# Softmax-normalisation hooks moved one or two steps later, and the second layer norm's pass on GpSimd in two of four blocks

## Chip, cores and metric

The kernel runs on one core of a Trainium2 chip. The metric is device time in microseconds (us), the median of several executions. A separate execution was recorded by the hardware profiler; durations below come from that one.

## What is computed

A transformer block whose two layer norms are modulated by a condition vector `c`, with attention of 32 query heads that share one key and one value head, and a bilinear feed-forward network:

```python
mod = silu(c) @ w_mod                       # six rows: sa, ca, ga, sb, cb, gb
h = layernorm(x) * (1 + ca) + sa
q = h @ wq (32 heads of 16);  k = h @ wk;  v = h @ wv
p = softmax(q k^T / 4);  o = p v
x = x + ga * (o @ wo)
h = layernorm(x) * (1 + cb) + sb
x = x + gb * (((h @ w_gate) * (h @ w_up)) @ w_down)
```

There are 2048 tokens, 512 model columns and 1792 feed-forward columns, all float32.

## The kernel before, in words

**Blocks and units.** The tokens are cut into four blocks of 512 queries (b = 0 to 3). In a block the 32 heads are done four at a time, so a block has 8 units and the program 32 (u = 0 to 31, g = u mod 8). A unit goes over 16 key tiles of 128 keys. One key tile is a *turn*, and a turn has two half-turns; the hooks that are called in them have the index i, 0 to 31 in a unit.

**What a turn does.** Four score products (`sc`, L631) whose exponentials ScalarE writes (`P`, L633); four score products of a later unit for the row maximum (`mx`, L581) that VectorE reduces (`mpart`, L584); and, one turn late, eight accumulating products of P with the values (`pv`, L642; the four heads of a pair of key tiles share the array by column groups). Eight PSUM banks are handed round among all of these.

**Side work.** In what is left of TensorE's time, half-height products are put between the others, in one row group of the array while `sc` or `mx` uses the other (`side`, L499): first the query projections of the later blocks (four slots in a turn, called FEW), then, from unit 8 on, the output projection (`wo`) and the feed-forward products of the block before (eight slots in a turn, called MANY). Where a `side` group changes its row group, its product waits, by a dependency written by hand, for an exponential of the turn before.

**Softmax normalisation.** When two units (8 heads) are done, their sums of exponentials lie in DRAM (`rs`). `normalise` then has three steps: `load` (SP reads the sums as a 128x32 tile `rc`, L664), `recip` (VectorE takes reciprocals, L667; SP writes them to DRAM as `ri`, L669, and reads them back, spread over the partitions, as `rr`, L671), and `mult` (GpSimd multiplies the head outputs `oc` by `rr`, L676, and splits the product into two float16 halves `och`, L678 and L679). `hooks` calls these in units with g in (0, 3, 4, 6), at i = 4, 8 and 14. The last group of the last block is normalised after the attention.

**Second layer norm.** Early in the next block (units 8 and 9, 16 and 17, 25 and 26) four `wo` groups, one for each token tile t of 128 tokens, end one after the other. At each end VectorE adds the residual (`x`, L724), takes statistics (`bs`, L732) and combines them (`st`, L735); GpSimd makes the reciprocal deviation in six tiny operations (`ry`, L190 to L195) and in two more the bias `nb` (L737, L738). After the fourth tile, the pass that writes the normalised tile (`n2`, here shown as `n`, L742) is called for t = 0 to 3 after 2, 4, 6 and 9 ticks in the later blocks, and the transposes (`mx`, L771), whose evictions are `hf` (L778), from tick 11 on. Two ticks make a turn. The pass is a ScalarE activation, n2 = y*x + nb.

**Order.** The program is written out in one order for all engines; each engine takes its own instructions in that order, and waits at one whose input or buffer isn't ready while everything behind it on that engine waits too. GpSimd also prepares the feed-forward weights (`wsl`, `kwb`, `wg`, `wu`, `wd`; L903 to L1010) until unit 11 or so, and splits the feed-forward products (`glu`, L824 and L825).

Of the kernel before, what the change touches and what calls it, by code (L numbers as in the profile page):

```python
# [15 lines left out]
AF = mybir.ActivationFunctionType  # L16
OP = mybir.AluOpType
# [22 lines left out]
CHANNEL = {0: KC - 1, 3: 0, 4: 1, 6: 2}  # L40
# [13 lines left out]
def adaln_mqa_glu_kernel(ctx: ExitStack, tc: tile.TileContext, x_in, wq_in, wk_in, wv_in, wo_in,  # L54
                         wg_in, wu_in, wd_in, c_in, wm_in, out):
    nc = tc.nc
# [140 lines left out]
    def rstd_of(st, n):  # L197
        y = work.tile([128, 4], F32, name="ry", bufs=6)[:, :n]
        rstd_into(y, st[:, :, 1], n)
        return y  # L200
# [487 lines left out]
    def after(delay, f):  # L688
        if tick[0] is None:
            f()  # L690
        else:
            timers.setdefault(tick[0] + delay, []).append(f)
# [6 lines left out]
    def load_x(b, t):  # L699
        xl = work.tile([128, D], F32, name="xl", tag="xl", bufs=3)  # L700
        r0 = b * BT + t * 128
        nc.sync.dma_start(xl, x_rows[r0:r0 + 128, :])
        xls[b, t] = xl

    def wo_work(b):
        def op(t):
            def f(i):
                ch, term = divmod(i, 3)
                ol, wl = TERMS[term]
                return och[b, ch][:, ol, t * 128:(t + 1) * 128], wo[:, wl, ch, :]  # L710
            return f

        def pre(t):
            def f():
                load_x(b, t)
            return f

        def fin(t):
            def f(p):
                if b < NB - 1:  # L720
                    x1 = work.tile([128, D], F32, name="x1", tag="x1", bufs=6)
                else:
                    x1 = work.tile([128, D], F32, name="x1p", tag="P", bufs=8)
                nc.vector.scalar_tensor_tensor(x1, p, sca[:, 7:8], xls[b, t], op0=OP.mult, op1=OP.add)  # L724
                x1s[b, t] = x1
                s2 = work.tile([128, 1, 2], F32, name="st2", bufs=5)
                bs = work.tile([128, 6], F32, name="bs", bufs=4)
                nb = work.tile([128, 2], F32, name="nb", bufs=4)
                yt = {}

                def spread():
                    nc.vector.bn_stats(bs, x1)  # L732

                def aggr():
                    nc.vector.bn_aggr(s2[:, 0, :], bs)  # L735
                    yt["y"] = rstd_of(s2, 1)
                    nc.gpsimd.tensor_tensor(nb[:, 0:1], s2[:, 0, 0:1], yt["y"], op=OP.mult)  # L737
                    nc.gpsimd.tensor_scalar(nb[:, 1:2], nb[:, 0:1], -1.0, 0.0, op0=OP.mult, op1=OP.add)  # L738

                def nrm():  # L740
                    n2 = work.tile([128, D], F32, name="n2", tag="och", bufs=4)
                    nc.scalar.activation(n2, x1, AF.Identity, bias=nb[:, 1:2], scale=yt["y"])  # L742
                    n2s[b, t] = n2

                after(3, spread)
                after(4, aggr)
                n2f[b, t] = nrm
                if t == 3:
                    for j, d in enumerate((2, 4, 6, 9) if b else (2, 4, 7, 12)):
                        after(d, n2f[b, j])  # L750
                    if b < NB - 1:
                        after(TR_WAIT if b else TR_WAIT + 3, lambda: turns.extend(ln2_work(b)))
            return f

        return [Group(3 * KC, op(t), fin(t), pre(t)) for t in range(4)]
# [5 lines left out]
    def ln2_work(b):  # L761
        items = []
        st = {}

        def tr(k):
            def f():
                if k == 0:
                    h2s[b] = big.tile([128, 2, KC, BT], F16, name="h2T", tag="wq")
                st["p"] = ps_hold("mx")
                for t in range(4):  # L770
                    nc.tensor.transpose(st["p"][:, t * 128:(t + 1) * 128], n2s[b, t][:, k * 128:(k + 1) * 128],  # L771
                                        ident)
            return f

        def ev(k):
            def f():
                hf = work.tile([128, BT], F32, name="hf", tag="g", bufs=2)
                nc.scalar.activation(hf, st["p"], AF.Identity, bias=hsc[:, k, 0:1], scale=hsc[:, k, 1:2])  # L778
                ps_give(st["p"])
                eng = nc.vector if b == NB - 1 else nc.gpsimd  # L780
                eng.tensor_scalar(h2s[b][:, 0, k, :], hf, 1.0, 0.0, op0=OP.mult, op1=OP.add)
                eng.tensor_tensor(h2s[b][:, 1, k, :], hf, h2s[b][:, 0, k, :], op=OP.subtract)
                if k == KC - 1:
                    h2done.add(b)
            return f

        for k in range(KC):
            items.append((900, tr(k), ev(k)))
        return items
# [310 lines left out]
    def side_step(step):  # L1100
        if side and step >= side_next[0] and (step % 2 or side[0][1] is nothing):
            gap, f, post = side.popleft()
            side_next[0] = max(side_next[0], step) + gap
            f()
            if post:
                posts.append(post)
# [26 lines left out]
    nrm = []  # L1133
# [16 lines left out]
    def attend(u, kt):  # L1150
# [9 lines left out]
        for turn in range(2):  # L1160
# [31 lines left out]
            if not late_max() and turns:  # L1192
                _, f, post = turns.popleft()
                f()
                posts.append(post)
            hooks(u, 2 * (kt + turn) + 1)

    def hooks(u, i):
        b, g = divmod(u, UB)
        step = u * NSTEP + i  # L1200
        side_step(step)
        if u > 0 and g in CHANNEL and i in (4, 8, 14):
            if i == 4:
                nrm[:] = normalise(b - (g == 0), CHANNEL[g])
            nrm[(4, 8, 14).index(i)]()
        if i == 16 and u > 0 and g == 0:
            left = list(fill)
            fill.clear()
            gu, down = ffn_work(b - 1)
            early = max(len(left) - 2, 0)  # L1210
            fill.extend(left[:early])
            fill.extend(([step + 4], w) for w in wo_work(b - 1))
            fill.extend(left[early:])
            fill.extend((["h2", b - 1], w) for w in gu + down)
# [14 lines left out]
    u = NU - 1  # L1229
# [28 lines left out]
    nrm = normalise(NB - 1, KC - 1)  # L1258
# [33 lines left out]
```

## Time and profile before

| What | us |
|---|---|
| Time, median of 3 runs (1699.13 to 1699.99) | 1699.75 |
| The profiled execution's own time | 1698.53 |
| Its span, first to last instruction | 1696.5 |
| TensorE matmul busy | 1653.9 |
| VectorE busy | 1392.2 |
| ScalarE busy | 1220.1 |
| GpSimd busy | 506.3 |

Rows of the profile give an engine's instructions in order of time: start, duration, engine, line, operation, output<-input, shapes and count, and in brackets how long the engine was idle just before and what released it. Grouped rows give busy time and the mean in ns of one instruction, then idle time. A wait row gives total us, number of times and the longest. Runs of equal instructions are merged in a timeline into one row, which starts with the first of them.

### The profile page before, as it was taken

What the parts mean: (1) busy time and instruction counts of PE and PEld (TensorE: products, weight loads), DVE (VectorE), ACT (ScalarE), POOL (GpSimd) and SP (SyncE); (2) the same over time, 40 slices, a digit from 0 to 9 for tenths busy, and PEclk for the clock granted to TensorE, in tenths of its full rate; (3) what the DMA queues carried; (4) which work ended last, traced back from release to release, by engine and by line L of the source; (5) the groups of instructions that cost most, each with busy time, mean ns of one, the idle gap of its engine ahead of it and who ended that gap; (6) DMA issues with size and microseconds to landing.
All of it is one profiled execution on the core that took longest, in us unless ns stands there. A gap on an engine that the chain in (4) does not pass through costs nothing.

```text
span 1696.5 us, 33291 instructions
## 1 busy us (share of the span) xinstructions
PE 1653.9 (97%) x12709; PEld 535.1 (32%) x12709; DVE 1392.2 (82%) x2364; ACT 1220.1 (72%) x2295; POOL 506.3 (30%) x705
## 2 busy tenths in 40 slices
PE   6799999999999999999999999999999999999999
PEld 3223333222223333333333333333323333334444
DVE  7799999999998999999989999999998999703110
ACT  3678888888887787777787778787777787772010
POOL 5724445535676751110020110101011111112130
PEclk9899999999999999999999999999999999999999
DMA  5212222311322210001100000000010000001000
GB/s 203 99 36 84 64 79 66 96 35 56 83 81 59 67 41 9 17 9 29 34 5 18 16 16 9 16 10 16 17 39 11 22 15 9 12 4 42 19 1 25
DMA packets 48939, 66.64 MB, mean 39 GB/s; under 512 B 15302, under 2 KB 29450, under 8 KB 48780
## 3 DMA queue, kind: packets, MB, share of 16 engines
q1 hardware_dynamic: 47196, 64.33, 12.6%
q8 instruction: 99, 1.62, 0.4%
q14 instruction: 60, 0.49, 0.1%
q10 hardware_dynamic: 1584, 0.20, 0.1%
HBM read 51.12 MB, written 8.92 MB: 35 GB/s over the span
## 4 chain that ended last, share of the span: by engine, by line
PE 86%; DVE 7%; ACT 3%; POOL 1%; issue 1%; DMA 1%; SPq 0%; ACTq 0%; POOLq 0%
PE side L499 49%; PE pv L642 27%; DVE mpart L584 7%; PE sc L631 5%; PE mx L581 3%; ACT P L633 2%; DMA wmA<-in_w_mod_dram 1%; POOL h L415 1%; PE mx L771 1%; PE pk L257 0%; PE pq L352 0%; PE mxt L608 0%; ACT kwb L250 0%; DMA rc<-rs 0%; PE sc L247 0%
## 5 line engine op out<-in xcount | busy, mean ns | idle before, releaser
L584 DVE TENSOR_REDUCE mpart<-mx 128x1 f32<-128x512 f32 x2016 | 1267.1, 683 | 100.3 <-PE mx L581 95.3
L633 ACT ACTIVATE P<-sc 128x512 f32<-128x512 f32 x2048 | 1092.4, 599 | 263.0 <-PE sc L631 219.0
L631 PE MATMUL sc<-sst,kst 50*128 50x512 f16 x2048 | 664.4, 379 | 1.1 <-DVE mpart L584 0.6
L581 PE MATMUL mx<-kst,sst 48*128 48x512 f16 x2032 | 616.5, 377 | 11.6 <-DVE mpart L584 5.5
L642 PE MATMUL pv<-P,vst 128*32 128x512 f32 x4096 | 546.2, 605 | 1.2
L499 PE MATMUL side<-h2T,wg 64*128 64x512 f16 (+1 forms) x1168 | 284.3, 378 | 0.0
L499 PE MATMUL side<-h2T,wu 64*128 64x512 f16 (+1 forms) x1166 | 282.9, 378 | 0.1
L499 PE MATMUL side<-wd,glu 64*128 64x512 f16 (+1 forms) x1008 | 234.1, 378 | 2.2 <-ACT P L633 2.2
L824 POOL TENSOR_SCALAR glu<-gf 128x512 f16<-128x512 f32 x56 | 34.7, 620 | 633.8 <-DVE gf L823 552.9
L631 PEld LDWEIGHTS <-kst 50*128 50x128 f16 x2048 | 175.7, 94 | 130.9 <-issue 109.4
L581 PEld LDWEIGHTS <-sst 48*128 48x128 f16 x2048 | 182.3, 94 | 68.3 <-issue 44.3
L499 PEld LDWEIGHTS <-wg 64*128 64x128 f16 (+1 forms) x1168 | 100.8, 94 | 202.3 <-ACT P L633 94.8
L499 PEld LDWEIGHTS <-wu 64*128 64x128 f16 (+1 forms) x1166 | 100.7, 95 | 200.0 <-ACT P L633 92.4
L642 PEld LDWEIGHTS pv<-P,vst 128*32 128x32 f32 x4096 | 80.8, 108 | 216.1 <-issue 200.0
L499 PEld LDWEIGHTS <-glu 64*128 64x128 f16 (+1 forms) x1008 | 89.1, 95 | 165.5 <-ACT P L633 65.5
L823 DVE TENSOR_TENSOR gf<-side,g 128x512 f32<-128x512 f32 x56 | 38.3, 685 | 115.9 <-PE side L499 82.5
L499 PE MATMUL side<-h,wq 64*128 64x512 f16 (+1 forms) x372 | 98.3, 382 | 0.0
L818 ACT ACTIVATE g<-side 128x512 f32<-128x512 f32 x56 | 33.2, 593 | 81.5 <-PE side L499 81.5
L499 PE MATMUL side<-wo,och 64*128 64x512 f16 (+1 forms) x336 | 79.3, 378 | 0.0
L825 POOL TENSOR_TENSOR glu<-gf,glu 128x512 f16<-128x512 f32 x56 | 65.0, 1160 | 4.7
L190 POOL TENSOR_SCALAR rv<-st 128x1 f32<-128x1 f32 (+1 forms) x20 | 4.6, 228 | 169.3 <-DVE st L735 154.0
L912 POOL TENSOR_TENSOR kwb<-kwb,wsl 128x448 f32<-128x448 f32 (+1 forms) x40 | 47.6, 1189 | 3.1
(221 smaller groups left out, 770.9 us busy)
## 6 DMA issues: line engine op xcount, KB each, us to landing
wsl<-in_B_w_gate_dram SPq DMA_DIRECT2D x32, 224.0 KB
wsl<-in_B_w_up_dram SPq DMA_DIRECT2D x32, 224.0 KB
wsl<-in_B_w_down_dram SPq DMA_DIRECT2D x28, 256.0 KB
sst<-qd SPq DMA_DIRECT2D x186, 32.0 KB
qd<-q SPq DMA_DIRECT2D x16, 256.0 KB
oc<-ev SPq DMA_DIRECT2D x128, 32.0 KB
rr<-ri SPq DMA_DIRECT2D x16, 256.0 KB
xl<-in_A_x_dram SPq DMA_DIRECT2D x16, 256.0 KB
```

Source lines behind the costliest of these rows:

```text
L415: nc.gpsimd.tensor_tensor(lo, t, hi, op=OP.subtract)
L499: return nc.tensor.matmul(self.p, left[64 * r0:64 * r1], right[64 * r0:64 * r1], start=start, stop=self.ended())
L581: nc.tensor.matmul(m, s[64 * a:64 * a + 48, p, t * 128:(t + 1) * 128], keys, start=True, stop=True)
L584: nc.vector.tensor_reduce(part, m, axis=AX.X, op=OP.max)
L631: nc.tensor.matmul(t, kst[64 * a:64 * a + 50, kt * 128:(kt + 1) * 128], s[64 * a:64 * a + 50, p, :], start=True, stop=True)
L633: ex = nc.scalar.activation(ptl[u, kt, p, a], t, AF.Exp)
L642: nc.tensor.matmul(pvb[u][32 * j:32 * j + 32, :], vst[:, kt, :], ptl[u, kt, p, a], start=(kt == 0), stop=(kt == KT - 1))
L818: nc.scalar.activation(st["g", f], p, AF.Copy, scale=2.0 ** -45)
L823: nc.vector.tensor_tensor(gf, p, st["g", f], op=OP.mult)
L824: nc.gpsimd.tensor_scalar(st["glu"][:, 0, f, :], gf, 1.0, 0.0, op0=OP.mult, op1=OP.add)
L825: nc.gpsimd.tensor_tensor(st["glu"][:, 1, f, :], gf, st["glu"][:, 0, f, :], op=OP.subtract)
L912: nc.gpsimd.tensor_tensor(acc, acc, t, op=OP.add)
```

## The change

The three steps of `normalise` are called at i = 5, 10 and 15. In blocks b = 1 and 2 the pass of the second layer norm is a GpSimd `tensor_scalar`, (x - mean) * y, and the two tiny GpSimd operations for the bias are left out; blocks 0 and 3 keep the ScalarE pass. Lines from L737 on have numbers 1 to 4 higher afterwards (the pass is then L744 on GpSimd and L746 on ScalarE).

```diff
                 def aggr():
                     nc.vector.bn_aggr(s2[:, 0, :], bs)
                     yt["y"] = rstd_of(s2, 1)
-                    nc.gpsimd.tensor_tensor(nb[:, 0:1], s2[:, 0, 0:1], yt["y"], op=OP.mult)
-                    nc.gpsimd.tensor_scalar(nb[:, 1:2], nb[:, 0:1], -1.0, 0.0, op0=OP.mult, op1=OP.add)
+                    if b not in (1, 2):
+                        nc.gpsimd.tensor_tensor(nb[:, 0:1], s2[:, 0, 0:1], yt["y"], op=OP.mult)
+                        nc.gpsimd.tensor_scalar(nb[:, 1:2], nb[:, 0:1], -1.0, 0.0, op0=OP.mult, op1=OP.add)
 
                 def nrm():
                     n2 = work.tile([128, D], F32, name="n2", tag="och", bufs=4)
-                    nc.scalar.activation(n2, x1, AF.Identity, bias=nb[:, 1:2], scale=yt["y"])
+                    if b in (1, 2):
+                        nc.gpsimd.tensor_scalar(n2, x1, s2[:, 0, 0:1], yt["y"], op0=OP.subtract, op1=OP.mult)
+                    else:
+                        nc.scalar.activation(n2, x1, AF.Identity, bias=nb[:, 1:2], scale=yt["y"])
                     n2s[b, t] = n2
...
-        if u > 0 and g in CHANNEL and i in (4, 8, 14):
-            if i == 4:
+        if u > 0 and g in CHANNEL and i in (5, 10, 15):
+            if i == 5:
                 nrm[:] = normalise(b - (g == 0), CHANNEL[g])
-            nrm[(4, 8, 14).index(i)]()
+            nrm[(5, 10, 15).index(i)]()
```

The first place is ScalarE in unit 17, block 1's second layer norm: P are exponentials, n the normalised tiles, mt a row of maxima, hf the evicted transposes. Before:

```order
L633 ACTIVATE P<-sc 128x512 x31
L742 ACTIVATE n_12895<-x_12435,nb,ry 128x512
L633 ACTIVATE P<-sc 128x512 x4
L742 ACTIVATE n_12956<-x_12586,nb,ry 128x512
L633 ACTIVATE P<-sc 128x512 x4
L742 ACTIVATE n_12998<-x_12728,nb,ry 128x512
L633 ACTIVATE P<-sc 128x512 x5
L742 ACTIVATE n_13061<-x_12867,nb,ry 128x512
L633 ACTIVATE P<-sc 128x512 x4
L613 ACTIVATE mt_13107<-mxt 16x128
```

ScalarE at the same place after the change:

```order
L648 ACTIVATE ev<-pv,evs 128x512
L633 ACTIVATE P<-sc 128x512 x48
L613 ACTIVATE mt_13099<-mxt 16x128
L633 ACTIVATE P<-sc 128x512 x4
L782 ACTIVATE hf<-mx,hsc 128x512
```

The four passes are gone, and 48 exponentials follow each other up to the row of maxima. They stand now on GpSimd, behind the deviations (rv to ry) of the third and fourth token tile and ahead of the split of the transposed tiles (h2T):

```order
L195 TENSOR_TENSOR ry<-ry,rt 128x1
L744 TENSOR_SCALAR n_12889<-x_12435,st_12437,ry 128x512
L190 TENSOR_SCALAR rv<-st_12863 128x1
L191 TENSOR_TENSOR ry<-rv,nhalf 128x1
L192 TENSOR_TENSOR rt<-ry 128x1
L193 TENSOR_TENSOR rt<-rt,rv 128x1
L194 TENSOR_SCALAR rt<-rt 128x1
L195 TENSOR_TENSOR ry<-ry,rt 128x1
L744 TENSOR_SCALAR n_12948<-x_12584,st_12586,ry 128x512
L744 TENSOR_SCALAR n_12990<-x_12724,st_12726,ry 128x512
L744 TENSOR_SCALAR n_13053<-x_12861,st_12863,ry 128x512
L785 TENSOR_SCALAR h2T<-hf 128x512
```

The first pass waits ahead of the fourth tile's deviation, and the other three follow it without anything between. The last place is VectorE in units 3 and 4, where the reciprocals stand among the maxima (cmq and mm are small reductions). Before:

```order
L925 TENSOR_REDUCE cmq<-mx 128x1
L584 TENSOR_REDUCE mpart<-mx 128x1 x18
L667 RECIPROCAL rc<-rc 128x32
L584 TENSOR_REDUCE mpart<-mx 128x1 x36
L601 TENSOR_REDUCE mm<-mpart 128x16
L584 TENSOR_REDUCE mpart<-mx 128x1 x2
L614 SCALAR_TENSOR_TENSOR mt_3505<-mxt,mt_3504 16x128
L584 TENSOR_REDUCE mpart<-mx 128x1 x26
L667 RECIPROCAL rc<-rc 128x32
L584 TENSOR_REDUCE mpart<-mx 128x1 x36
```

VectorE at the same place after the change:

```order
L929 TENSOR_REDUCE cmq<-mx 128x1
L584 TENSOR_REDUCE mpart<-mx 128x1 x22
L667 RECIPROCAL rc<-rc 128x32
L584 TENSOR_REDUCE mpart<-mx 128x1 x32
L601 TENSOR_REDUCE mm<-mpart 128x16
L584 TENSOR_REDUCE mpart<-mx 128x1 x2
L614 SCALAR_TENSOR_TENSOR mt_3505<-mxt,mt_3504 16x128
L584 TENSOR_REDUCE mpart<-mx 128x1 x30
L667 RECIPROCAL rc<-rc 128x32
L584 TENSOR_REDUCE mpart<-mx 128x1 x32
```

Each reciprocal stands four maxima, one turn, later. TensorE's instructions keep their order throughout. On SP one or two weight loads go ahead of `ri` and `rr` in units 3, 4, 8 and 11, and on GpSimd a query split (L529, L530) goes ahead of the multiplication in unit 3.

## Prediction

> **What bounds the kernel now.** I read the page's busy times and its chain first, then the waits of TensorE and VectorE in the stretches that the change touches, then their timelines.
>
> ```profile
> PE 1653.9 (97%) x12709; PEld 535.1 (32%) x12709; DVE 1392.2 (82%) x2364; ACT 1220.1 (72%) x2295; POOL 506.3 (30%) x705
> ...
> POOL 5724445535676751110020110101011111112130
> ...
> PE 86%; DVE 7%; ACT 3%; POOL 1%; issue 1%; DMA 1%; SPq 0%; ACTq 0%; POOLq 0%
> ```
>
> TensorE is busy for 97% of the span and carries 86% of the chain (the second row, GpSimd's busy tenths in 40 slices of 42.4 us, is used further down). So an edit is worth only what TensorE now waits for, plus what VectorE loses where it is full. TensorE's idle time is 1696.5 - 1653.9 = 42.6 us in all. This change moves no instruction of TensorE; so the question is which of its waits go. Two groups of rows answer.
>
> The first is TensorE's timeline in unit 17, where block 1's second layer norm is passed over. `pv` comes once in a turn, so the distance from one `pv` to the next is the length of a turn.
>
> ```profile
> 854.98 1.07 PE L642 MATMUL pv<-P,vst 128*32 128x512 f32 x8
> ...
> 857.84 1.07 PE L642 MATMUL pv<-P,vst 128*32 128x512 f32 x8
> 859.25 0.39 PE L499 MATMUL side<-wd,glu 64*128 64x512 f16 x1 [0.34 <-ACT P L633]
> ...
> 861.09 1.06 PE L642 MATMUL pv<-P,vst 128*32 128x512 f32 x8
> 862.56 0.39 PE L499 MATMUL side<-wd,glu 64*128 64x512 f16 x1 [0.40 <-ACT P L633]
> ...
> 864.39 1.06 PE L642 MATMUL pv<-P,vst 128*32 128x512 f32 x8
> 865.83 0.39 PE L499 MATMUL side<-wd,glu 64*128 64x512 f16 x1 [0.37 <-ACT P L633]
> ...
> 867.67 1.07 PE L642 MATMUL pv<-P,vst 128*32 128x512 f32 x8
> ...
> 870.51 1.06 PE L642 MATMUL pv<-P,vst 128*32 128x512 f32 x8
> ```
>
> The turns last 2.86, 3.25, 3.30, 3.28 and 2.84 us. In the three long ones the first side product behind `pv` waits for an exponential, 0.34 + 0.40 + 0.37 = 1.11 us together. ScalarE's groups say why the exponential is late:
>
> ```profile
> L633 ACT ACTIVATE P<-sc 128x512 f32<-128x512 f32 x2048 | 1092.4, 599 | 263.0 <-PE sc L631 219.0 <-PE mx L581 37.1 <-ACT P L633 0.4
> ...
> L742 ACT ACTIVATE n<-x,nb,ry 128x512 f32<-128x512 f32 x12 | 9.8, 818 | 0.0
> ```
>
> Four exponentials and one pass are 4 x 0.60 + 0.82 = 3.22 us, more than a turn of 2.84 us: with the pass in it ScalarE sets the turn, and without it (2.4 us) it doesn't. The same three waits stand in unit 26, for block 2:
>
> ```profile
> 1267.41 0.39 PE L499 MATMUL side<-wd,glu 64*128 64x512 f16 x1 [0.34 <-ACT P L633]
> ...
> 1270.72 0.39 PE L499 MATMUL side<-wd,glu 64*128 64x512 f16 x1 [0.40 <-ACT P L633]
> ...
> 1273.99 0.39 PE L499 MATMUL side<-wd,glu 64*128 64x512 f16 x1 [0.38 <-ACT P L633]
> ```
>
> That is 1.12 us more. The fourth pass of each block costs nothing now: behind 864.39 the turns are 3.28 (the third pass) and then 2.84 us, although the fourth runs there.
>
> The second group is VectorE's timeline at the reciprocals of units 3, 4 and 6, with the number of idle us in brackets.
>
> ```profile
> 225.74 0.35 DVE L667 RECIPROCAL rc<-rc 128x32 f32<-128x32 f32 x1 [0.77 <-DMA rc<-rs]
> ...
> 267.14 0.35 DVE L667 RECIPROCAL rc<-rc 128x32 f32<-128x32 f32 x1 [0.69 <-DMA rc<-rs]
> ...
> 348.78 0.34 DVE L667 RECIPROCAL rc<-rc 128x32 f32<-128x32 f32 x1
> ```
>
> In units 3 and 4 VectorE stands still until the sums have landed, in unit 6 it doesn't. VectorE is full there: of this stretch of 83 us (busy us of TensorE, its weight loads, VectorE, ScalarE, GpSimd) it works for 81.11.
>
> ```profile
> 172.00:255.00 83.00, 82.46 (x676) 26.12 (x674) 81.11 (x137) 70.14 (x138) 40.84 (x43) 1.00 0.24 72
> ```
>
> and TensorE's `pv` rows show the loss as time:
>
> ```profile
> 224.73 1.07 PE L642 MATMUL pv<-P,vst 128*32 128x512 f32 x8
> 228.18 1.06 PE L642 MATMUL pv<-P,vst 128*32 128x512 f32 x8
> 230.68 1.07 PE L642 MATMUL pv<-P,vst 128*32 128x512 f32 x8
> ...
> 266.21 1.07 PE L642 MATMUL pv<-P,vst 128*32 128x512 f32 x8
> 269.59 1.07 PE L642 MATMUL pv<-P,vst 128*32 128x512 f32 x8
> ```
>
> The turns with the reciprocal last 3.45 and 3.38 us, the next one 2.50: 0.95 and 0.88 us too long. Of that 0.77 and 0.69 are the wait, and some 0.18 each is the reciprocal itself.
>
> **The change part by part.**
>
> *Pass off ScalarE.* Eight activations go (8 x 0.82 = 6.5 us of ScalarE). What TensorE gains is the six waits: 1.11 + 1.12 = 2.23 us by the idle times; by the turns it is 3.25 + 3.30 + 3.28 - 3 x 2.84 = 1.31 us in a block, 2.62 in both. Next late would be VectorE:
>
> ```profile
> 852.87 3.36 DVE L584 TENSOR_REDUCE mpart<-mx 128x1 f32<-128x512 f32 x5
> ...
> 856.15 0.74 DVE L724 SCALAR_TENSOR_TENSOR x<-side,sca,xl 128x512 f32<-128x512 f32 x1
> 856.80 2.48 DVE L584 TENSOR_REDUCE mpart<-mx 128x1 f32<-128x512 f32 x4
> 859.20 0.68 DVE L732 BATCH_NORM_STATS2 bs<-x 128x6 f32<-128x512 f32 x1
> ...
> 863.21 2.56 DVE L584 TENSOR_REDUCE mpart<-mx 128x1 f32<-128x512 f32 x4 [0.75 <-PE mx L581]
> ```
>
> It runs without a pause from 852.87 to 862.46 and pauses for 0.75 us in the turn after. Four maxima take 2.48 us of the 2.84, and the fourth tile's residual and statistics come on top, so a turn or so will be a little over 2.84. I take 1.15 us in a block, just above the idle sum, 2.3 us in both; bounds 2.2 and 2.6.
>
> *Pass on GpSimd.* The trace has no such operation. The nearest rows are GpSimd's scalar multiplication in float32 over 448 columns and its two-input product over 512:
>
> ```profile
> L1008 POOL TENSOR_SCALAR wsl<-wsl,sca 128x448 f32<-128x448 f32 x32 | 20.6, 642 | 12.2 <-DMA wsl<-in_B_w_gate_dram 7.5 <-DMA wsl<-in_B_w_up_dram 4.6
> ...
> L676 POOL TENSOR_TENSOR oc<-oc,rr 128x512 f32<-128x512 f32 x5 | 6.4, 1277 | 7.9 <-DMA wsl<-in_B_w_up_dram 3.8 <-DMA rr<-ri 3.4 <-DMA wsl<-in_B_w_down_dram 0.7
> ```
>
> So a pass takes 0.64 to 1.28 us; the one-input row is nearer (0.64 x 512/448 = 0.73). It costs nothing as long as four are done before the transposes:
>
> ```profile
> 860.76 0.22 POOL L190 TENSOR_SCALAR rv<-st 128x1 f32<-128x1 f32 x1 [6.37 <-DVE st L735]
> ...
> 876.11 0.62 POOL L781 TENSOR_SCALAR h2T<-hf 128x512 f16<-128x512 f32 x1 [12.82 <-ACT hf L778]
> ```
>
> The first pass can run in the 6.4 us of idle time ahead of the last deviation, the other three behind it, from about 862.8 to 865 (or 866.6 at 1.28 us). GpSimd then has nothing until the first transposed tile at 876.11, so its cover is some 8 us. The two tiny operations that go (16 in all) lay in the same idle time: nothing.
>
> *Hooks.* Even if the sums land a whole half-turn (2.50 / 2 = 1.25 us) later because `load` is called later, `recip`, two half-turns later, gains 1.25 us on them, more than the longest wait of 0.77. Gain: 0.77 + 0.69 = 1.46 us; up to 0.95 + 0.88 = 1.83 if the reciprocal itself hides too, as in unit 6; down to nothing if VectorE, full there, loses as much at the new place. I take 1.5. The other reciprocals either had their sums or stand beside a TensorE that sets the pace: 0.
>
> *What comes later for it.* `ri` and `rr` leave up to 2.5 us later, `mult` is called 1.25 to 1.4 us later. On GpSimd its wait for `rr` stays about as long, with squares of the weights queued behind. Their next reader is TensorE's sum:
>
> ```profile
> 284.08 1.14 POOL L912 TENSOR_TENSOR kwb<-kwb,wsl 128x448 f32<-128x448 f32 x1
> ```
>
> ```profile
> 290.81 0.40 PE L922 MATMUL mx<-kwb,onec 128*32 128x112 f32 x8
> ```
>
> The last square ends 290.81 - 285.22 = 5.6 us ahead of the sum, over twice the delay: 0. SP's loads that overtake `ri` only come sooner: 0. The `och` halves are read by `wo` from i = 20 on at the earliest, while `mult` at 15 is three operations of at most 1.28 us each, done by i = 18: 0.
>
> **Sum.** 2.3 + 1.5 = 3.8 us off the profiled execution's 1698.53 (span 1696.5 and 2.0 around it) gives 1694.7. The median of the runs is 1.2 us above that execution, so I forecast 1699.75 - 3.8 = 1695.95, say 1695.9. With the bounds (3.7 to 4.4 where both parts hold, and some loss by VectorE) its own range is 1695.2 to 1696.8. A measurement can tell about 0.2%, 3.4 us, so the forecast lies just beyond that line, at 1696.35.
>
> **Rivals.**
>
> 1. *VectorE takes over in units 17 and 26.* If its unbroken stretch of 9.6 us is the real limit, a wait for `mpart` replaces the wait for P, and only the reciprocals' 1.5 us stay: 1698.2. For it: no pause up to 862.46. Against it: the pauses of 0.75 us directly behind, in turns that ScalarE makes long.
>
> 2. *The reciprocal loses as much at its new place,* because VectorE is full in units 3 and 4: only 2.3 us stay, 1697.4. Against it: unit 6, where a reciprocal without a wait left no idle time.
>
> 3. *GpSimd's passes stop VectorE: slower.* If the two can't use the tile memory at once, each pass holds up VectorE for its length, in turns where VectorE has no time to give: 8 x 0.64 to 1.28 = 5.1 to 10.2 us lost against 3.8 gained, 1701.0 to 1706.1, middle 1703.6. It decides once more than 3.8 us of the passes land on VectorE's queue. Against it stand VectorE's maxima in two stretches:
>
> ```profile
> L584 DVE TENSOR_REDUCE mpart<-mx 128x1 f32<-128x512 f32 x125 | 79.3, 685 | 8.7 <-PE mx L581 8.7
> ```
>
> ```profile
> L584 DVE TENSOR_REDUCE mpart<-mx 128x1 f32<-128x512 f32 x128 | 81.3, 685 | 7.7 <-PE mx L581 7.7
> ```
>
> The first is 510 to 600 us, where GpSimd is 60 to 70% busy by the page's slices (the 13th and 14th), the second 692 to 784, where it is under 20% (the 17th to 19th): 685 ns in both. But residual and statistics, which read the tile memory, had no such test. The Trainium skill (Advanced Engine Details and Errata, section VectorE Performance Modes, Mode Summary) says that the second Vector port to that memory is shared with GpSimd, and that GpSimd instructions and two-port Vector instructions block each other. By that rule the maxima, which have a PSUM input, are free, as the trace agrees, and the rival keeps only the residual and statistics.
>
> 4. *Part of it doesn't do what it says:* GpSimd falls behind by more than the 5.6 us in unit 4 (2 us lost, 1697.9), or the waits stay as they are (1699.7).
>
> **How the numbers follow.** Forecast 0.66; rival 1 0.10, rival 2 0.10, rival 3 0.06, rival 4 0.08. Three quarters of the forecast lie beyond 3.4 us: faster 0.50; slower is rival 3, 0.06; the rest, 0.44, is within 0.2%. The range takes in the forecast and rivals 1 and 2 (0.86): 1695.0 to 1698.4.
>
> **What would show it.** In unit 17 and 26: no side product with a wait for P, turns of 2.84 to 2.95 us at those places, L744 on GpSimd at 0.64 to 1.28 us. In units 3 and 4: reciprocals without idle time, turns of about 2.7 us. Wrong if `side` or `mx` waits for `mpart` there instead, if statistics or residual grow beyond 0.68 and 0.74 us, or if TensorE waits for `kwb`.

## The result, and the profile after

| Kernel | Median us (lowest to highest, runs) | Profiled execution's time | Its span |
|---|---|---|---|
| before | 1699.38 (1695.18 to 1699.99, 7) | 1698.53 | 1696.5 |
| after | 1693.31 (1690.21 to 1695.78, 7) | 1690.55 | 1688.5 |

The ratio is 0.9967, with an interval of 0.9956 to 0.9977: faster by 3.9 to 7.5 us. The direction was forecast; the time lies 2.6 us under the forecast and 1.7 under the range. The page of the kernel after has TensorE again at the end of nearly everything: busy time of each engine, then the chain.

```profile
PE 1650.2 (98%) x12709; PEld 534.5 (32%) x12709; DVE 1391.9 (82%) x2364; ACT 1214.8 (72%) x2287; POOL 519.9 (31%) x697
...
PE 88%; DVE 7%; ACT 2%; POOL 2%; issue 1%; DMA 1%; SPq 0%; ACTq 0%; POOLq 0%
```

**The span fell by 8.0 us, and that isn't all the change.** I cut the span at an instruction ahead of all moved work, the eviction of unit 1's values (L648, the second one). It starts at 176.35 us before and at 172.97 after. No instruction of this head is changed, so its 3.4 us must have another source. The windows view shows it (busy time of five engines, then TensorE's granted clock, the DMA share and GB/s); before:

```profile
40.00:60.00 20.00, 16.33 (x65) 7.21 (x64) 15.19 (x27) 13.59 (x25) 12.11 (x22) 0.91 0.42 158
60.00:90.00 30.00, 23.32 (x156) 6.08 (x156) 22.08 (x55) 18.50 (x38) 26.24 (x32) 0.89 0.21 63
90.00:120.00 30.00, 29.54 (x226) 8.59 (x225) 29.02 (x48) 23.62 (x47) 7.26 (x7) 0.94 0.07 22
```

and after:

```profile
40.00:60.00 20.00, 14.70 (x65) 6.71 (x64) 16.75 (x29) 15.15 (x27) 13.01 (x23) 1.00 0.42 158
60.00:90.00 30.00, 25.45 (x166) 6.42 (x169) 23.11 (x58) 19.32 (x40) 28.44 (x34) 0.89 0.22 70
90.00:120.00 30.00, 29.95 (x252) 9.36 (x246) 29.77 (x51) 23.46 (x47) 4.06 (x4) 1.00 0.05 16
```

The records give the clock as 1.0 or 0.5, in stretches of 3.4 us: four of them at half before (13.6 us: 0.5 x 3.4 of 20 us is the 0.91, 0.5 x 6.8 of 30 us the 0.89), two after (6.8 us). Half of the 6.8 us between them is the 3.4. That is an argument from the sizes, and it holds only roughly: over the fourteen traces of this study the cut lies at 172.8 to 173.0 us with two such stretches ahead of it, at 175.3 with three, 176.3 to 177.0 with four, 175.0 to 175.5 with five and 177.2 to 177.7 with six. What the change is worth must be read from the **main part**, from that eviction to the end: 1520.16 before, 1515.50 after, so 4.66 us.

**Unit 17.** TensorE's timeline after, where the three waits for P stood:

```profile
849.51 1.06 PE L642 MATMUL pv<-P,vst 128*32 128x512 f32 x8
852.35 1.06 PE L642 MATMUL pv<-P,vst 128*32 128x512 f32 x8
855.33 1.06 PE L642 MATMUL pv<-P,vst 128*32 128x512 f32 x8
858.17 1.06 PE L642 MATMUL pv<-P,vst 128*32 128x512 f32 x8
861.00 1.07 PE L642 MATMUL pv<-P,vst 128*32 128x512 f32 x8
863.84 1.06 PE L642 MATMUL pv<-P,vst 128*32 128x512 f32 x8
866.89 1.06 PE L642 MATMUL pv<-P,vst 128*32 128x512 f32 x8
867.88 0.66 PE L775 MATMUL mx<-ident,n 128*128 128x128 f32 x4
```

No product waits now. The first five turns take 14.33 us (849.51 to 863.84) where the same five took 15.53 (854.98 to 870.51). Measured between the exponentials, unit 17 is 1.18 us shorter, and unit 26 also 1.18. TensorE's waits between the cut and the end of the attention, before:

```profile
PE mx L581 <- DVE mpart L584: 4.8, 21, 0.4
PE side L499 <- ACT P L633: 2.2, 6, 0.4
PE mxt L608 <- DVE mm L601: 1.7, 3, 0.8
```

and after:

```profile
PE mx L581 <- DVE mpart L584: 3.8, 17, 0.2
PE mxt L608 <- DVE mm L601: 1.7, 3, 0.8
```

The six waits for P are gone and none for `mpart` has come in their place; rather, four of those went too.

**The pass on GpSimd is not what I had priced.** GpSimd's timeline in unit 17, from the first pass to the split of the first transposed tile:

```profile
848.33 2.11 POOL L744 TENSOR_SCALAR n<-x,st,ry 128x512 f32<-128x512 f32 x1
...
857.12 6.22 POOL L744 TENSOR_SCALAR n<-x,st,ry 128x512 f32<-128x512 f32 x3
869.44 0.62 POOL L785 TENSOR_SCALAR h2T<-hf 128x512 f16<-128x512 f32 x1 [6.11 <-ACT hf L782]
```

A pass takes 2.09 us (the mean of eight), above my upper bound of 1.28. It cost nothing only because the last one ends at 863.34, 4.5 us ahead of the transposes at 867.88.

**The reciprocals.** VectorE in units 3 and 4, after:

```profile
224.01 0.34 DVE L667 RECIPROCAL rc<-rc 128x32 f32<-128x32 f32 x1
...
264.63 0.35 DVE L667 RECIPROCAL rc<-rc 128x32 f32<-128x32 f32 x1
```

Neither has idle time in front of it. TensorE's `pv` rows around the first:

```profile
221.35 1.07 PE L642 MATMUL pv<-P,vst 128*32 128x512 f32 x8
223.86 1.06 PE L642 MATMUL pv<-P,vst 128*32 128x512 f32 x8
226.45 1.06 PE L642 MATMUL pv<-P,vst 128*32 128x512 f32 x8
```

The turn that now holds the reciprocal lasts 2.59 us, the one ahead of it 2.51; neither is near the 3.45 of before. By the exponentials unit 3 is 0.85 us shorter and unit 4 1.07, and five later units (11, 14, 19, 22, 30) 0.12 each, which I had at 0.

### The profile page after: what moved, and what is told of

Its sections match the earlier page's. It is cut to its first block, busy times and chain, and to the rows that moved or that the text cites. A ratio compares the mean times of both kernels' runs of the same rounds, so it can differ in the third digit from the quotient of the medians.

```text
span 1688.5 us, 33275 instructions
## 1 busy us (share of the span) xinstructions
PE 1650.2 (98%) x12709; PEld 534.5 (32%) x12709; DVE 1391.9 (82%) x2364; ACT 1214.8 (72%) x2287; POOL 519.9 (31%) x697
## 4 chain that ended last, share of the span: by engine, by line
PE 88%; DVE 7%; ACT 2%; POOL 2%; issue 1%; DMA 1%; SPq 0%; ACTq 0%; POOLq 0%
PE side L499 50%; PE pv L642 28%; DVE mpart L584 6%; PE sc L631 5%; PE mx L581 3%; ACT P L633 1%; POOL h L415 1%; DMA wmA<-in_w_mod_dram 1%; PE mx L775 1%; PE pk L257 0%; PE pq L352 0%; PE mxt L608 0%; ACT kwb L250 0%; POOL wq L415 0%; PE sc L247 0%
## 5 line engine op out<-in xcount | busy, mean ns | idle before, releaser
L676 POOL TENSOR_TENSOR oc<-oc,rr 128x512 f32<-128x512 f32 x15 | 19.2, 1280 | 109.9 <-DMA sst<-qd 50.8
```

The source lines that it names most:

```text
L676: eng.tensor_tensor(o, o, st["r"], op=OP.mult)
```

## The experiments

Theory A is the prediction's: ScalarE's waits and the waits for the sums go, GpSimd's passes are hidden by their lead on the transposes. The main parts of all profiled executions, in us:

| Kernel | Main part | Median us (lowest to highest, runs) | Ratio to before |
|---|---|---|---|
| before / before again | 1520.16 / 1521.35 | 1698.59 again (1695.55 to 1701.12, 11) | 0.9997 [0.9988, 1.0007] |
| after / after again | 1515.50 / 1515.54 | 1692.95 again (1690.39 to 1694.61, 5) | 0.9962 [0.995, 0.9975] |
| hooks only | 1517.71 | 1692.58 (1692.17 to 1696.94, 5) | 0.9968 [0.9956, 0.9981] |
| pass only | 1518.40 | 1696.61 (1693.43 to 1698.36, 11) | 0.9985 [0.9976, 0.9994] |
| `recip` only, at 10 | 1517.92 | 1696.53 (1693.03 to 1697.55, 10) | 0.9984 [0.9974, 0.9993] |
| `recip` only, at 9 | 1519.01 | 1695.95 (1693.41 to 1698.83, 10) | 0.9981 [0.9972, 0.9991] |
| `load` and `mult` only | 1520.09 | 1698.93 (1696.06 to 1700.5, 10) | 1.0000 [0.999, 1.0009] |
| three blocks | 1518.70 | 1697.82 (1694.58 to 1698.25, 10) | 0.9993 [0.9984, 1.0002] |
| pass twice | 1520.47 | 1697.38 (one) | - |
| four forms | 1515.44 | 1690.32 (one) | - |
| three blocks, transposes later | 1516.34 | 1694.27 (1690.89 to 1695.64, 8) | 0.9966 [0.9955, 0.9977] |
| multiply and add | 1515.17 | 1692.7 (1690.63 to 1694.31, 5) | 0.9964 [0.995, 0.9978] |

The times of one kernel spread over some 5 us, mostly with the half-clock stretches of the head, so the main part and the turns in it tell more than a median. By its median of five runs the kernel with the hooks only looks as fast as the full change, but its interval (3.2 to 7.5 us gained) is too wide to tell, and its main part is 2.2 us longer.

### The hooks alone

The pass stays on ScalarE in all blocks, the hooks are at 5, 10 and 15. Against the kernel before:

```diff
-        if u > 0 and g in CHANNEL and i in (4, 8, 14):
-            if i == 4:
+        if u > 0 and g in CHANNEL and i in (5, 10, 15):
+            if i == 5:
                 nrm[:] = normalise(b - (g == 0), CHANNEL[g])
-            nrm[(4, 8, 14).index(i)]()
+            nrm[(5, 10, 15).index(i)]()
```

> Only the three hooks are moved; the second layer norm's pass stays on ScalarE in all blocks. Main part = from the eviction of unit 1's values (line 648, in unit 2) to the end of the span; head = all before it. Theory A (two separate gains, and the rest of the measured 6 us is the head, where the granted clock drops to half in some stretches of 3.4 us at times that differ from run to run): the main part is 2.2 us shorter than before (0.86 in unit 3, 1.07 in unit 4, and some 0.3 in units 11 to 31); units 17 and 26 keep their turns of 3.25 to 3.30 us. Rival B (the two edits help each other, or the change as a whole shortens the head): the main part gains clearly less than 2.2 us here, under 1.5, or the head is 2 us or more shorter in every profile of a changed kernel.

Main part 1517.71: 2.45 less than before. The waits for P are back in unit 17 as they were; TensorE's timeline:

```profile
853.55 0.39 PE L499 MATMUL side<-wd,glu 64*128 64x512 f16 x1 [0.34 <-ACT P L633]
...
856.86 0.39 PE L499 MATMUL side<-wd,glu 64*128 64x512 f16 x1 [0.40 <-ACT P L633]
...
860.13 0.39 PE L499 MATMUL side<-wd,glu 64*128 64x512 f16 x1 [0.37 <-ACT P L633]
```

Unit 3 gains 0.86, unit 4 1.07 and the five later units 0.12 each: 2.53, where the prediction had 1.5. So the hooks hold the larger part of the error.

### The pass alone

The hooks are back at 4, 8 and 14. Against the kernel after:

```diff
-        if u > 0 and g in CHANNEL and i in (5, 10, 15):
-            if i == 5:
+        if u > 0 and g in CHANNEL and i in (4, 8, 14):
+            if i == 4:
                 nrm[:] = normalise(b - (g == 0), CHANNEL[g])
-            nrm[(5, 10, 15).index(i)]()
+            nrm[(4, 8, 14).index(i)]()
```

> Only the pass is moved to GpSimd in the second and third block; the hooks stay at 4, 8 and 14. Theory A: the main part is 2.4 us shorter than before (1.2 in unit 17 and 1.2 in unit 26), and the reciprocals of units 3 and 4 still wait 0.7 to 0.8 us. Rival B: clearly another number, under 1.8 or over 3, or a head shorter by 2 us or more.

Units 17 and 26 are 1.18 us shorter each, as in the full change: the two parts add. But the main part is only 1.76 below that of before, not 2.36, just under the 1.8 where rival B of this run began; but what B meant, another gain in the two units or a head shorter by 2 us, isn't there. Unit 4 is 0.37 us longer than before, though nothing is changed there. VectorE's timeline shows why:

```profile
224.86 0.35 DVE L667 RECIPROCAL rc<-rc 128x32 f32<-128x32 f32 x1 [0.76 <-DMA rc<-rs]
...
266.65 0.35 DVE L667 RECIPROCAL rc<-rc 128x32 f32<-128x32 f32 x1 [1.07 <-DMA rc<-rs]
```

The wait in unit 4 was 0.69 in the first profile. The wait that the hooks remove isn't the same in every execution. The rest of the difference is smaller: units 8, 20, 25 and 28 are 0.10 to 0.12 longer each and unit 24 is 0.12 shorter. In units 20, 24, 25 and 28 it is so in the kernel after too; how the pass does that I have not followed.

### Both kernels again

The kernels before and after, each unchanged, to see how much one execution's waits are worth.

> The kernel before, unchanged. Theory A: the main part is the same as in the first profile within 0.3 us; the head and with it the whole time differ by up to 5 us from run to run, and the time goes with the mean granted clock: 0.1% of clock is some 1.7 us. Rival B: head and main part both as in the first profile, and times within 1 us of 1699.4.

> The changed kernel, unchanged. Theory A: main part 4.6 us shorter than before within 0.3 us, head anywhere within 5 us; at the same mean granted clock its time is 4.6 us below that of the kernel before. Rival B: the head is again 3 us or more shorter than that of the kernel before, and the difference at equal clock is about 6 us.

The kernel before, profiled again:

```profile
226.82 0.35 DVE L667 RECIPROCAL rc<-rc 128x32 f32<-128x32 f32 x1 [0.55 <-DMA rc<-rs]
269.18 0.35 DVE L667 RECIPROCAL rc<-rc 128x32 f32<-128x32 f32 x1 [1.65 <-DMA rc<-rs]
432.12 0.35 DVE L667 RECIPROCAL rc<-rc 128x32 f32<-128x32 f32 x1 [0.29 <-DMA rc<-rs]
```

Unit 4 waits 1.65 us this time and is 0.96 longer, unit 8 waits too and is 0.38 longer; the main part is 1.19 longer, where theory A of that run allowed 0.3. The changed kernel's main part came out the same to 0.04 us. So the hooks take away a loss that varies: in three executions with the old hooks (before twice, the pass alone) the grouped rows of the reciprocal have 2.7, 3.8 and 3.2 us of idle time, in the changed kernel 1.0, all of it behind the attention. That row, in the kernel after:

```profile
L667 DVE RECIPROCAL rc<-rc 128x32 f32<-128x32 f32 x16 | 5.5, 344 | 1.0 <-DMA rc<-rs 1.0
```

By the three pairs of main parts (before less hooks alone, before again less hooks alone, pass alone less after) the hooks are worth 2.45, 3.64 and 2.90 us.

The variation isn't in when the sums' load is issued. SP's row for it in unit 4, in the kernel before, and then in the kernel before profiled again:

```profile
264.46 0.33 SPq L664 DMA_DIRECT2D rc<-rs  x1
```

```profile
265.54 0.33 SPq L664 DMA_DIRECT2D rc<-rs  x1
```

Both stand 5.0 us behind the eviction of the values that the sums come with (L648). From there to the reciprocal, which starts when the sums have landed, it is 2.68 us in the first and 3.64 in the second, and 3.07 with the pass alone: the time behind the issue varies. In the kernel after the reciprocal of unit 4 starts 4.40 us behind the issue (260.23 to 264.63), later than the latest of these landings.

### Which hook it is

In the next three the pass is on ScalarE in all blocks and only some hooks move; the edits are against the kernel before.

```diff
-        if u > 0 and g in CHANNEL and i in (4, 8, 14):
+        if u > 0 and g in CHANNEL and i in (4, 10, 14):
             if i == 4:
                 nrm[:] = normalise(b - (g == 0), CHANNEL[g])
-            nrm[(4, 8, 14).index(i)]()
+            nrm[(4, 10, 14).index(i)]()
```

> Hooks at 4, 10 and 14: only the reciprocal's step is moved; the pass stays on ScalarE. Theory A (all that the hooks bring is that VectorE no longer stands at a reciprocal for sums that have not landed): the main part is as with the three hooks moved, 1517.7 us within 0.4, and no reciprocal under way has idle time ahead of it. Rival (GpSimd's and SP's new order, from load and mult one half-turn later, brings a share): the main part keeps 0.5 us or more of what separates it from the kernel before.

With `recip` at 10 and the other two in their old places, no reciprocal of the attention waits. All the gain of the hooks is there but 0.29 us in the last turn of unit 4 (the main part is 0.21 above that of the hooks alone, inside the 0.4 that theory A allowed).

```diff
-        if u > 0 and g in CHANNEL and i in (4, 8, 14):
+        if u > 0 and g in CHANNEL and i in (4, 9, 14):
             if i == 4:
                 nrm[:] = normalise(b - (g == 0), CHANNEL[g])
-            nrm[(4, 8, 14).index(i)]()
+            nrm[(4, 9, 14).index(i)]()
```

> Hooks at 4, 9 and 14: the reciprocal's step one half-turn later, 1.25 us in units 3 and 4 and 1.4 us later on. Theory A: waits up to 1.25 us go, longer ones (1.65 us was seen in unit 4) keep the difference, 0.4 us at most; the main part lies at 1517.7 to 1518.6 us and may differ from run to run. Rival (the place among the maxima matters, not the wait): the main part stays near that of the kernel before, 1520 to 1521.4.

One half-turn isn't enough in this execution: unit 4 keeps a wait.

```profile
267.46 0.35 DVE L667 RECIPROCAL rc<-rc 128x32 f32<-128x32 f32 x1 [0.18 <-DMA rc<-rs]
```

That turn is 0.36 us longer than with `recip` at 10, and units 11, 14, 19, 22 and 30 are 0.17 us longer each, without any wait for the sums. So in those units it is the reciprocal's place among VectorE's maxima that counts, a gain that I had put at zero since there is no wait there. The main part, 1519.01, lies between the theories of this run (up to 1518.6, and from 1520): each had a part of it.

```diff
-        if u > 0 and g in CHANNEL and i in (4, 8, 14):
-            if i == 4:
+        if u > 0 and g in CHANNEL and i in (5, 8, 15):
+            if i == 5:
                 nrm[:] = normalise(b - (g == 0), CHANNEL[g])
-            nrm[(4, 8, 14).index(i)]()
+            nrm[(5, 8, 15).index(i)]()
```

> Hooks at 5, 8 and 15: load and mult one half-turn later, the reciprocal where it was. Theory A: nothing is gained; where the later load delays the sums, the reciprocals wait up to 1.25 us longer each. The main part is 1520.2 to 1524 us, and the waits of units 3 and 4 are 0.7 us or longer. Rival (GpSimd's and SP's order brings a share): the main part is 0.5 us or more below 1520.2.

The main part is 1520.09 and the ratio 1.0000: the waits for the sums stay, and only the 0.28 us in unit 4's last turn come from here. In the kernel before, ScalarE's first exponential of that turn, behind the eviction of a query projection, starts after 0.34 us of idle time, and here it doesn't; what it waited for is not known. The later call of `load` doesn't delay the load: in unit 4 SP issues it 4.98 us behind the eviction, against 4.97 before. `load` and `mult` by themselves are worth nothing that can be timed.

### GpSimd's cover

Three blocks, not two, have their pass on GpSimd. Against the kernel after:

```diff
-                    if b not in (1, 2):
+                    if b == NB - 1:
...
-                    if b in (1, 2):
+                    if b < NB - 1:
```

> The changed kernel with the pass on GpSimd in the first block too. There GpSimd works without a pause on the feed-forward weights up to the transposes, and a pass takes 2.09 us on it, not the 0.64 to 1.28 that were assumed. Theory A (the pass is free only under GpSimd's idle time): the transposes of unit 9 wait for the last pass, and the main part is 2 to 8 us longer than the changed kernel's 1515.5. Rival (the pass is free anywhere off ScalarE): 1515.5 or up to 0.8 us less, since the passes lengthen three turns of unit 9 by about 0.25 us.

Block 0's passes (at 482.1, 486.7, 493.6 and 498.0) stand between the splits of the weights, and the last one is late. TensorE:

```profile
497.55 0.55 PE L775 MATMUL mx<-ident,n 128*128 128x128 f32 x3
500.15 0.33 PE L775 MATMUL mx<-ident,n 128*128 128x128 f32 x1 [2.05 <-POOL n L744]
502.13 1.86 PE L642 MATMUL pv<-P,vst 128*32 128x512 f32 x8
503.93 1.12 PE L775 MATMUL mx<-ident,n 128*128 128x128 f32 x4
```

Unit 9 is 3.22 us longer than in the kernel after. The wait itself is 2.05 of it. Behind it the eight `pv` products take 1.86 us in place of 1.06, and four transposes 1.12 in place of 0.66: the windows show the clock before and behind the wait.

```profile
498.00:502.00 4.00, 1.72 (x10) 0.54 (x9) 1.20 (x4) 1.49 (x3) 3.83 (x5) 1.00 0.22 59
502.00:506.00 4.00, 4.00 (x20) 1.35 (x20) 1.59 (x4) 2.16 (x5) 3.75 (x6) 0.57 0.21 59
```

So a stretch at half clock followed a wait of 2 us; whether it always does, one trace can't say.

Next the pass is written twice in blocks 1 and 2, with the same result.

```diff
                         nc.gpsimd.tensor_scalar(n2, x1, s2[:, 0, 0:1], yt["y"], op0=OP.subtract, op1=OP.mult)
+                        nc.gpsimd.tensor_scalar(n2, x1, s2[:, 0, 0:1], yt["y"], op0=OP.subtract, op1=OP.mult)
```

> The changed kernel, with each pass of blocks 1 and 2 written a second time on GpSimd (the same result, twice the GpSimd work). Theory A (GpSimd's lateness counts only beyond its cover of 4.5 us before the first transposes): eight passes of 2.09 us end some 6.2 us after four would have, 1.8 us behind the transposes' place: a wait of TensorE of 1.5 to 2.5 us in unit 17 and in unit 26 for n from GpSimd, main part (from the eviction of unit 1's values to the end) 1518.5 to 1520.5 against 1515.5. Rival B (GpSimd's passes take a port from VectorE): VectorE's residuals, statistics or maxima beside the passes get longer by over 5% (the residual 743 ns, statistics 686 ns, maxima 684 ns), and the turns from the first pass on are longer, not only the one with the transposes. Rival C (the cover is longer than the rows say): no change.

TensorE in unit 17:

```profile
869.86 0.55 PE L776 MATMUL mx<-ident,n 128*128 128x128 f32 x3
871.86 0.33 PE L776 MATMUL mx<-ident,n 128*128 128x128 f32 x1 [1.46 <-POOL n L745]
```

Unit 17 is 1.68 us longer, in the one turn that holds the transposes; the wait in unit 26 is 1.66, and there a half-clock stretch follows it, so that unit is 3.35 longer. The wait came out just below the 1.5 to 2.5 that A gave it in unit 17, and rival C is out. The main part, 1520.47, lies at the upper end of A's range only with the half-clock stretch in it, which A didn't have. This run is also the test of rival B, GpSimd stopping VectorE, that the kernel after couldn't give, since no residual and no statistics of VectorE lie inside its passes. Here one does. GpSimd's second pass, with the first of VectorE's rows beneath it:

```profile
852.52 2.08 POOL L745 TENSOR_SCALAR n<-x,st,ry 128x512 f32<-128x512 f32 x1
```

```profile
852.63 0.74 DVE L724 SCALAR_TENSOR_TENSOR x<-side,sca,xl 128x512 f32<-128x512 f32 x1
853.28 2.48 DVE L584 TENSOR_REDUCE mpart<-mx 128x1 f32<-128x512 f32 x4
```

The residual runs wholly inside the pass and takes 0.74 us as ever (742 ns). With three blocks the statistics stood inside a pass, from 482.13 to 484.23, and took their 0.68:

```profile
482.72 0.68 DVE L732 BATCH_NORM_STATS2 bs<-x 128x6 f32<-128x512 f32 x1
```

### Why a pass takes 2.09 us

Each token tile of blocks 1 and 2 has another form of the pass; tile 2 is as it was, and the other three leave out a part of the normalisation. The lines in place of the one pass:

```diff
+                        if t == 0:
+                            nc.gpsimd.tensor_scalar(n2, x1, yt["y"], 0.0, op0=OP.mult, op1=OP.add)
+                        elif t == 1:
+                            nc.gpsimd.tensor_scalar(n2, x1, s2[:, 0, 0:1], 1.0, op0=OP.subtract, op1=OP.mult)
+                        elif t == 2:
+                            nc.gpsimd.tensor_scalar(n2, x1, s2[:, 0, 0:1], yt["y"], op0=OP.subtract, op1=OP.mult)
+                        else:
+                            nc.gpsimd.tensor_scalar(n2, x1, 0.5, 0.25, op0=OP.subtract, op1=OP.mult)
```

> The changed kernel, with four different forms of the pass in blocks 1 and 2, one for each token tile: tile 0 multiplies by the reciprocal root only (one scalar from memory, one constant; leaves out subtracting the mean), tile 1 subtracts the mean only (one from memory, one constant; leaves out the scale), tile 2 as it was (two from memory), tile 3 has two constants (leaves out both). The pass took 2.09 us, where the weights' scaling of 128x448 with one scalar from memory takes 0.64. Theory A (the second scalar from memory costs it): tiles 0, 1 and 3 take 0.70 to 0.80 us, tile 2 2.09. Rival B (the subtraction costs it): tiles 1, 2 and 3 take 2.1 us, tile 0 0.73. Rival C (it is the buffers or the shape, not the scalars): all four take 2.1 us. Time as the changed kernel's, since the passes end earlier still: main part 1515.0 to 1516.0.

The grouped rows (busy us, then mean ns of one; L745 is tile 0, L747 tile 1, L749 tile 2, L751 tile 3):

```profile
L749 POOL TENSOR_SCALAR n<-x,st,ry 128x512 f32<-128x512 f32 x2 | 4.2, 2082 | 0.0
L747 POOL TENSOR_SCALAR n<-x,st 128x512 f32<-128x512 f32 x2 | 4.1, 2028 | 0.0
L751 POOL TENSOR_SCALAR n<-x 128x512 f32<-128x512 f32 x2 | 3.8, 1924 | 0.0
L745 POOL TENSOR_SCALAR n<-x,ry 128x512 f32<-128x512 f32 x2 | 1.4, 694 | 0.0
```

Theory A of that run, the second scalar from memory, falls: with two constants it is still 1.92 us. It is the form subtract-then-multiply, rival B; multiply-then-add takes 0.69. Whether the subtraction costs it or the order of the two operations was not tried apart. The main part is 1515.44, as the kernel after's: passes that end earlier still give nothing more.

### Two versions that might do better

Three blocks again, with block 0's transposes three half-turns later, so that the last pass lies ahead of them. Beside the edit for three blocks:

```diff
-                            after(TR_WAIT if b else TR_WAIT + 3, lambda: turns.extend(ln2_work(b)))
+                            after(TR_WAIT if b else TR_WAIT + 6, lambda: turns.extend(ln2_work(b)))
```

> The passes of three blocks on GpSimd, as before, with the transposes of block 0 three half-turns later, so that GpSimd's fourth pass (which ended at 500.1 us) lies ahead of them. Theory A (only the lost cover cost the 3.2 us): no wait of TensorE for n from GpSimd in unit 9, main part 1515.0 to 1515.8 (the changed kernel 1515.5, less some 0.5 for the two waits for ScalarE in unit 9 that go). Rival B (the weights' splits that the passes delay cost as much elsewhere): waits for wg, wu or h2T in units 9 to 13, main part 1516.5 to 1519.

No wait of TensorE for `n` is left in unit 9, but the main part is 1516.34, between what A and B gave. The turns up to the last exponential are 0.9 us shorter in sum than the kernel after's; what lies behind it is 1.72 longer, because more of the side work's products are left over by then (752 in place of 744; 16 fewer are done in unit 9). Neither theory had that: a later transpose delays the side work that follows from it, to the end.

Last, the hooks as changed, with the cheap form in blocks 0 to 2 (y and nb from memory; the two tiny operations for `nb` stay). Against the kernel before, the hooks' lines left out:

```diff
-                    nc.scalar.activation(n2, x1, AF.Identity, bias=nb[:, 1:2], scale=yt["y"])
+                    if b < NB - 1:
+                        nc.gpsimd.tensor_scalar(n2, x1, yt["y"], nb[:, 1:2], op0=OP.mult, op1=OP.add)
+                    else:
+                        nc.scalar.activation(n2, x1, AF.Identity, bias=nb[:, 1:2], scale=yt["y"])
```

> Hooks at 5, 10 and 15, and the passes of blocks 0, 1 and 2 on GpSimd in another form: multiplied by the reciprocal root and added to nb, both from memory, in place of mean subtracted and then multiplied; transposes at their old places. In the four forms tried, the one that multiplies and adds with one scalar from memory took 0.69 us, and all three that subtract and multiply took 1.92 to 2.08, with two, one or no scalar from memory. Theory A (the form subtract-multiply costs it, not the second scalar): passes of 0.65 to 0.80 us in all three blocks, no wait of TensorE for n from GpSimd in unit 9, main part (from the eviction of unit 1's values to the end) 1514.5 to 1515.3 against the changed kernel's 1515.5, since unit 9 loses its waits for ScalarE (0.5) and gets none for GpSimd. Rival B (a second scalar from memory costs as much in this form too): passes of about 2.1 us and unit 9 some 3.2 us longer, main part about 1518.7, as with three blocks in the old form.

```profile
L743 POOL TENSOR_SCALAR n<-x,ry,nb 128x512 f32<-128x512 f32 x12 | 9.1, 765 | 0.0
```

0.765 us, inside theory A's range, and no wait for `n` in unit 9. The main part is 1515.17, 0.33 below the kernel after's: unit 9 gives 0.32 of it. Its median, 1692.7, can't be told from 1693.31. So this version beats the kernel before, and the kernel after by no more than its trace shows.

## Why the prediction was right or wrong

**Pass off ScalarE: right.** Forecast 1.15 us in a block, 1.18 measured in both, with and without the hooks. VectorE did not take over (rival 1): the turns are 2.83 to 2.98 us. By the main parts (hooks alone less after) the pass is worth 2.21 us, since units 20, 25 and 28 lose and unit 24 gains some 0.1 each: the lower end of the bounds of 2.2 to 2.6.

**Pass on GpSimd: nothing lost, as forecast, but the price was outside its bounds.** 2.09 us against 0.64 to 1.28. I had taken a row of the same operation, TENSOR_SCALAR, and let the kind of arithmetic in it pass; it decides (0.69 or 2.08 on the same tile). The three later passes took 3 x 2.08 = 6.2 us in place of 2.2 by my 0.73, which ate 4.0 of the cover; 4.5 were left. Writing the passes twice used those up, and TensorE waited.

**The reciprocals: the failing step.** The prediction put them at "0.77 + 0.69 = 1.46 us; up to 0.95 + 0.88 = 1.83", and "the other reciprocals ... 0". The mechanism held: the waits went, nothing came at the new place (rival 2 is out), and `recip` by itself does nearly all of it. The later landing that the prediction allowed for didn't come: the load is issued where it was. The size was off in three ways. Against the same execution, the two turns with the reciprocal in units 3 and 4 gave 0.95 and 0.87 us and the turns behind them took back 0.09 each: 1.64, between my value and my upper end. Five later units gave 0.6 without any wait there, and unit 4's last turn 0.28, which comes with `load` and `mult` and whose cause is open. Together 2.5. And I had read the wait from one execution, as if it were a constant of the kernel: in others it is up to 1.1 us longer in sum, so the hooks are worth 2.5 to 3.6. With 2.2 for the pass that makes 4.7 to 5.9 us; the two ratios of the change, 0.9967 and 0.9962, give 5.6 and 6.5, with intervals that hold the one and the other.

**What comes later for it: nothing, as forecast.** The last square `kwb` ends 3.9 us ahead of TensorE's sum (281.94 to 285.79), 5.6 before, and TensorE has no wait for it.

**Rival 3, GpSimd stops VectorE: not so, and now tested on the rows it named.** The Trainium skill (Advanced Engine Details and Errata, section VectorE Performance Modes, Mode Summary) says that the second Vector port is shared with GpSimd and that the two block each other when VectorE uses it. By that rule only an instruction that uses both ports can be held up; the residual and the statistics, each inside a GpSimd pass, kept 0.74 and 0.68 us, so no run here shows such a block. The prediction let the maxima off for their PSUM input and passed over that the residual has one too (`side`); the statistics, which read and write the tile memory alone, are the closer test.

**The base.** I subtracted from a median of three runs, 1699.75, and let the range reach only 0.9 us below the forecast. Single executions of either kernel spread over 5 us. In a straight-line fit over all runs of this study, a granted clock higher by 0.001 goes with 0.9 us less (I had expected 1.7); at equal clock the kernel after is 5.6 us below the one before, give or take 0.6 (theory A, when it was run again, had 4.6, from one pair of traces). That agrees with the parts, 4.7 to 5.9. So of the miss of 2.6 us the reciprocals are 1.0 to 2.1, the base some 0.4 (1699.38), and the rest is within the scatter of the medians: luck of the executions drawn. Why the sums' transfer takes longer in some executions was not tried.

## What to carry to other kernels

A wait for a small DMA has to be read from several executions before it is priced: here it was 0.69 to 1.65 us at one and the same instruction, and calling that two half-turns later took it away in all nine traces that have it there. On an engine that is full, the place of a small instruction counts even where it waits for nothing, so such turns are compared one by one rather than put at zero. When work goes to another engine, price it by a row with the same arithmetic, not only the same operation name, and compare the sum with the lead on the first reader, which is worth nothing until it is used up.

## What was not expected of the hardware

GpSimd's `tensor_scalar` on 128x512 float32 takes 0.69 us when it multiplies and then adds (0.765 with both scalars from memory), but 1.92 to 2.08 when it subtracts and then multiplies, wherever the scalars are.

The clock dropped to half for 3.4 us after TensorE had stood still for 2.05 us in one place and 1.66 in another, and didn't after 1.46 us. In the second place the granted clock was 0.73 from 1280 to 1284 us, and the turn behind the wait was 1.48 us longer for it. The Trainium skill (TensorE: Matmul & The Clock Gate, Part 1) says that the clock is set by windows of about 3.4 us that run freely, so that the same kernel meets them at different points from run to run. The trace agrees as far as it goes: stretches of 3.4 us or twice that, from two to six times 3.4 us in the head of one kernel or another, at places that differ between two executions of the kernel before. In every trace they begin a whole number of 3.41 us apart: 50.86, 61.10 and 91.82 us in the kernel before, the last two 3 and 12 times that behind the first.
